# Products with v: two pairs of heads in every second unit, and the PSUM banks shared out again

## The chip, the core and the metric

One core of a Trainium2 chip runs one program. The metric is the device time of one execution in microseconds (us). Engines are named as in the profile: PE is TensorE's matmul, PEld its weight load, DVE is VectorE, ACT is ScalarE, POOL is GpSimd, SP is SyncE, which here only issues DMAs. PSUM, in which PE's results land, has eight banks; each holds 512 float32 in every partition.

## The reference

Attention with mixing of heads before and after the softmax (4 batches, 12 heads, 448 positions, head size 64), followed by a bilinear feed-forward layer:

```python
scores = scale * np.matmul(q, k.transpose(0, 1, 3, 2))
scores = np.einsum('bhij,hg->bgij', scores, w_pre)
scores = scores - np.max(scores, axis=-1, keepdims=True)
attn = np.exp(scores)
attn = attn / (np.sum(attn, axis=-1, keepdims=True) + 1e-09)
attn = np.einsum('bhij,hg->bgij', attn, w_post)
...
x = attn_out.transpose(0, 2, 1, 3).reshape(B * S, H * D)
...
a = x @ w_a
b = x @ w_b
return (a * b @ w_out).astype(np.float32)
```

## The kernel before

The first part of the kernel, up to about 360 us, is the attention. The queries of a batch are cut into chunks of 120, 120, 120 and 88, and a chunk into **units** of 20 queries (the last unit of a batch has 8). That makes 23 units a batch and 92 in all. A loop over steps (L780) runs one step for each unit, and every engine works through its instructions in the order in which this loop writes them. Step s writes, on PE:

1. `premix(s)` (L306): the heads of unit s are mixed; four matmuls, recorded as eight, into two PSUM tiles `mp`, each for 10 queries. The order is half tile 0, half tile 1, half tile 0, half tile 1. The tiles come from the pool's tag `m`, which has three banks and hands them out in turn.
2. one `qk` (L259): the scores of one pair of heads for a later chunk, eight recorded matmuls into the tile `pst`, which has one buffer of two banks.
3. `av` (L386): the product with v for one pair of heads p, 16 recorded matmuls, for a **group** of six units (120 queries; the last group of a batch has five units and 88 queries). Three pairs share the PSUM tile `xp`, p = 0 to 2 and p = 3 to 5; it has the tag `x`, which has one bank. After p = 2 and p = 5 DVE copies `xp` to `xs` (L407), and SP stores it.
4. `postmix(s-1)` (L353): the weights of unit s-1 are mixed after the softmax; 64 recorded matmuls into the two tiles `pp`, one bank each.

ACT and DVE serve this in the same step. ACT first runs `evac_p(s-2)` (L368), two copies that empty `pp`. Then for each of the two tiles `mp` DVE takes the row maximum `nm` (L327), and ACT takes the exponential `a` with the row sums (L330). The exponential is the last reader of `mp`, and so what frees its bank. ACT or DVE then empties `pst` (L278 on DVE; L280 on ACT for every third pair of heads). `norm(s)` on DVE makes the scaled mixing matrix `kr` that `postmix(s)` reads, one step later. POOL issues the DMAs that bring the mixed rows `sb` (L297) four units ahead.

The places of the products with v are a table: pair p of a group that begins with unit u0 and has n units stands in step u0 + n + `AV_AT[p]`, or `AV_SHORT[p]` for a group of five. With the old tables every step from 7 to 93 has one pair, but for the steps 25, 48 and 71, which have two. Over the whole attention there are 90 such pairs in this loop (15 groups of six); the last group comes after it.

The eight banks are: `pp` two, `pst` two, `x` one, `m` three. Besides `mp`, the tag `m` serves four `psq` tiles at the start (scores of the first chunks, L269), the sums of the last group (`xp` with a == NA - 1), and in the second part of the kernel `pa` (L599) and every second `po` (L636).

From 360 us on, the feed-forward layer runs: products `pa` and `pb` in turn, then `po`, three matmuls of 448 columns for each term.

Of the kernel before, what the change touches and what calls it, by code (L numbers as in the profile page):

```python
# [7 lines left out]
F32 = mybir.dt.float32  # L8
# [13 lines left out]
def talking_heads_bilinear_kernel(  # L22
# [12 lines left out]
    B, _, G, S = k.shape  # L35
# [14 lines left out]
    CW = KD * 128  # L50
    KH = KD // 2
    AH = 4
    AV_AT = (1, 2, 3, 4, 5, 6)
    AV_SHORT = (2, 2, 3, 4, 5, 6)
    WARM = 40
    WARM3 = 24
    QK_EARLY = 4
# [34 lines left out]
    NA = len(groups)  # L92
# [9 lines left out]
    ps = ctx.enter_context(tc.tile_pool(name="ps", bufs=2, space=PSUM))  # L102
# [28 lines left out]
    def later(fn, n=3):  # L131
        todo_at.setdefault(now[0] + n, []).append(fn)
# [15 lines left out]
    def warm_up(n):  # L148
        if not n:
            return  # L150
        t = ps.tile([128, 512], F32, tag="x", name="warm", bufs=1)
        for i in range(n):
            nc.tensor.matmul(t[:, :128], lhsT=ones, rhs=ones)

# [42 lines left out]
    st, sbt, mt, at, rss, krs, ptt, xps = {}, {}, {}, {}, {}, {}, {}, {}  # L197
# [27 lines left out]
    def cut(n):  # L225
        nb, rest = divmod(n, QB)
        return QH * nb + min(rest, QH)
# [19 lines left out]
    def qk_head(c, i, g, out):  # L247
        b, t0, n = chunks[c]
        rows = slice(D * g, D * g + D)
        h0 = cut(n)  # L250
        for e in range(2):
            cols = slice(0, 64) if e == 0 else slice(h0, n)
            nc.tensor.matmul(  # L253
                out[64 * e:64 * e + cols.stop - cols.start],
                lhsT=qt[c, i // QG][rows, i % QG, cols],
                rhs=kt[b, i][rows],
            )

    def qk(c, i, own=1):  # L259
        b, t0, n = chunks[c]  # L260
        m = 64 + n - cut(n)
        if c not in st:
            st[c] = (k_p if c % 3 == 2 else big).tile([128, H, S], F32, tag="s", name="s", bufs=1 if c % 3 == 2 else 2)
        if c <= 1 and i % 2 and i < QK_EARLY + 2 * (1 - c):
            for g in range(2):
                if i == 3:
                    sp = pp_t[g].rearrange("p x j t -> p (x j t)")[:, :S]
                else:
                    sp = ps.tile([128, 512], F32, tag="m", name="psq", bufs=3)[:, :S]  # L269
                qk_head(c, i, g, sp)  # L270
                nc.vector.tensor_copy(st[c][:m, g * G + i], sp[:m])
            return
        sp = ps.tile([128, 2, 512], F32, tag="t", name="pst", bufs=1)[:, :, :S]
        for g in range(2):
            qk_head(c, i, g, sp[:, g])
        to = st[c].rearrange("p (g i) s -> p i g s", g=2)[:m, i]
        if own:
            nc.vector.tensor_copy(to, sp[:m])  # L278
        else:
            nc.scalar.copy(to, sp[:m])  # L280

    def halves(n):
        return [(o, min(QH, n - o)) for o in range(0, n, QH)]
# [15 lines left out]
    def blocks_of(u):  # L299
        n = units[u][2]  # L300
        return [(u, j, min(QB, n - QB * j)) for j in range(2) if n > QB * j]
# [4 lines left out]
    def premix(u):  # L306
        n = units[u][2]
        tiles = sbt.pop(u)
        for k_ in blocks_of(u):
            mt[k_[:2]] = ps.tile([128, 512], F32, tag="m", name="mp", bufs=3)[:, :S]  # L310
        for i in (0, 2, 1, 3):
            if i >= len(halves(n)):
                continue
            m = halves(n)[i][1] * H
            r, col = 64 * (i // 2), 64 * (i % 2)
            M = 64 if n == QU or i == 0 else m
            nc.tensor.matmul(mt[u, i // 2][col:col + M], lhsT=wp[r:r + m, :M], rhs=tiles[i % 2][r:r + m])  # L317
# [68 lines left out]
    def av(a, p):  # L386
        b, u0, _ = groups[a]
        t0 = (u0 - b * NUB) * QU
        n = min(AVC, S - t0)
        g = p // 3  # L390
        if p % 3 == 0:
            xp = ps.tile([128, 512], F32, tag="m" if a == NA - 1 else "x", name="xp", bufs=3 if a == NA - 1 else 1)
            xps[g] = xp[:, :3 * AVC].rearrange("p (a t) -> p a t", a=3)
        xp = xps[g]
        for r in range(R):
            for e in range(2):
                h = 2 * p + e
                nc.tensor.matmul(  # L398
                    xp[64 * e:64 * e + 64, p % 3, :n],
                    lhsT=vt[b % 2][g][:C2, h % G, r],  # L400
                    rhs=ptt[a][:C2, r, h, :n],
                    start=(r == 0),
                    stop=(r == R - 1),
                )
        if p % 3 == 2:
            xs = x_p.tile([128, 3, AVC], F32, tag="xs", name="xs")
            nc.vector.tensor_copy(xs[:, :, :n], xp[:, :, :n])  # L407
            later(lambda: nc.sync.dma_start(out=xd[b][:, 3 * g:3 * g + 3, t0:t0 + n], in_=xs[:, :, :n]), 1)
# [5 lines left out]
    for c in range(1, NC):  # L414
        b, t0, _ = chunks[c]
        for i in range(G):
            j = (c - 1) * G + i
# [9 lines left out]
    for a in range(NA):  # L427
        b, u0, n = groups[a]
        for p in range(H // 2):
            av_at[a, p] = u0 + n + (AV_AT if n == GU else AV_SHORT)[p]  # L430
            if a < NA - 1:
# [146 lines left out]
    def product(f, b, e, o, k0, k1):  # L578
        hh, ll = wt["a"] if f == e == 0 else wt["f", f]
        x, off = xt[b], 0 if f == e == 0 else e * KD  # L580
        for k in range(k0, k1):
            first, last = k == 0, k == KD - 1
            nc.tensor.matmul(o, lhsT=hh[:, off + k], rhs=x[:, 0, k], start=first, stop=False)  # L583
            nc.tensor.matmul(o, lhsT=hh[:, off + k], rhs=x[:, 1, k], start=False, stop=False)  # L584
            nc.tensor.matmul(o, lhsT=ll[:, off + k], rhs=x[:, 0, k], start=False, stop=last)  # L585
# [10 lines left out]
        later(lambda: nc.sync.dma_start(out=hd[b][:, f], in_=hf), 1)  # L596

    def run_a(f, b):
        pa = ps.tile([128, 512], F32, tag="m", name="pa", bufs=3)[:, :S]  # L599
        product(f, b, 0, pa, 0, KD)  # L600
        take_a(f, b, pa)

# [29 lines left out]
    def run_o(j):  # L632
        b, m = divmod(j, KD)
        hh, ll = wt.pop(("o", j))
        th, tl = ht[b]
        po = ps.tile([128, 512], F32, tag="m" if j % 2 == 0 else f"p{j // 2 % 2}", name="po", bufs=3 if j % 2 == 0 else 1)[:, :S]  # L636
        mm3(po, hh, ll, th, tl, KF)
        so = sb_p.tile([128, S], F32, tag="sb1", name="so")
        n = S // QU * QU
        for e in range(2):  # L640
            nc.scalar.copy(
                so[:, :n].rearrange("p (u j e t) -> p u j e t", j=2, e=2, t=QH)[:, :, :, e],
                po[:, :n].rearrange("p (u e j t) -> p u e j t", j=2, e=2, t=QH)[:, :, e],
            )
        if n < S:
            nc.scalar.copy(so[:, n:], po[:, n:])
        nc.sync.dma_start(out=out[m * 128:(m + 1) * 128, b * S:(b + 1) * S], in_=so)
# [89 lines left out]
    with tc.manual_schedule():  # L737
# [6 lines left out]
        load_k(0, 3)  # L744
        act_table()
        warm_up(WARM)
        setup_mask()
        clear_v(0)
# [142 lines left out]
        for j in range(B * KD):  # L891
            b, m = divmod(j, KD)
# [57 lines left out]
```

## Time and profile before

| | |
|---|---|
| Time, median of 3 runs | 895.96 us (891.77 to 896.65) |
| Profiled execution: time | 885.13 us |
| Profiled execution: span from first to last instruction | 883.4 us |
| PE busy in the span | 862.3 us (98%) |
| DVE, ACT, POOL busy | 516.5, 376.8, 440.9 us |
| Attention loop with one pair of heads in a step (units 7 to 82) | 45.64 to 322.29 us |
| Attention loop without `qk` (units 83 to 91) and what is left of the products with v | 322.29 to some 366 us |
| Mean granted TensorE clock | 0.999 of full speed |

The profile is of one execution. A row of the timeline gives a start in us from the span's beginning and a duration in us, and merges neighbouring instructions of one kind (xcount). A matmul's recorded end is modelled, so distances are taken from start to start. PE is busy nearly throughout; what a step costs is therefore the distance from one `premix` to the next.

### The profile page before, as it was taken

The numbers are of one execution on the slowest core, as the hardware profiler recorded it, in microseconds if no ns is written. First come the engines' busy times: TensorE is split into PE (matmuls) and PEld (weight loads), VectorE is DVE, ScalarE is ACT, GpSimd is POOL, SyncE is SP. The second block draws the span as 40 slices with busy tenths as digits, with TensorE's granted clock in tenths as the row PEclk, the third lists the DMA queues.
The fourth block names the chain that finished last, engine by engine and source line by source line (L and its number), as shares of the span: only waits on it lengthen the run. The fifth ranks groups of instructions, "written<-read, shape, count | busy, mean of one in ns | idle before, by whom it ended". The sixth has DMA issues, their size and how long they took to land.

```text
span 883.4 us, 27343 instructions
## 1 busy us (share of the span) xinstructions
PE 862.3 (98%) x11440; PEld 697.7 (79%) x11440; DVE 516.5 (58%) x913; ACT 376.8 (43%) x849; POOL 440.9 (50%) x549
## 2 busy tenths in 40 slices
PE   8799999999999899999999999999999999999998
PEld 4466566566566566899999999999999989999997
DVE  5577677667777685677755566555753545151500
ACT  5677677767677677431111111111111435353421
POOL 3786868587677762044432243233322255555552
PEclk9999999999999999999999999999999999999999
DMA  7776787676777964744433333333431674747441
GB/s 203 191 201 166 198 197 189 166 197 182 199 175 196 218 173 98 235 173 164 166 122 128 131 133 138 121 121 121 139 121 50 245 263 139 264 147 269 143 144 53
DMA packets 83172, 147.47 MB, mean 167 GB/s; under 512 B 42694, under 2 KB 63026, under 8 KB 82026
## 3 DMA queue, kind: packets, MB, share of 16 engines
q1 hardware_dynamic: 54922, 108.05, 37.9%
q0 software_dynamic: 28128, 37.68, 17.3%
q8 instruction: 90, 1.47, 0.7%
q14 instruction: 32, 0.26, 0.1%
HBM read 80.23 MB, written 26.74 MB: 121 GB/s over the span
## 4 chain that ended last, share of the span: by engine, by line
PE 91%; DMA 2%; DVE 2%; ACT 1%; issue 1%; SPq 1%; POOL 1%; ACTq 0%; DVEq 0%; POOLq 0%
PE pp L362 10%; PE xp L398 10%; PE mp L317 8%; PE pst L253 8%; PE po L573 6%; PE po L574 6%; PE po L572 6%; PE pa L583 6%; PE pa L585 6%; PE pa L584 6%; PE pb L585 6%; PE pb L584 6%; PE pb L583 6%; DMA sb<-s 1%; DMA k<-in_k_dram 1%
## 5 line engine op out<-in xcount | busy, mean ns | idle before, releaser
L297 POOL DMA_DIRECT2D sb<-s x350 | 202.1, 596 | 46.1 <-PE mp L317 22.0
L524 POOL TENSOR_TENSOR cvm<-cvm,cvr 128x768 int32<-128x768 int32 (+1 forms) x37 | 66.7, 1802 | 205.3 <-DVE cvm L523 205.3
L562 POOL TENSOR_TENSOR wl<-v,wh 128x768 fp32r<-128x768 f32 x48 | 93.4, 1966 | 100.7 <-ACT wh L561 100.7
L327 DVE TENSOR_REDUCE nm<-mp 124x1 f32<-124x448 f32 x180 | 104.0, 618 | 62.5 <-PE mp L317 61.7
L330 ACT ACTIVATE a<-mp,nm 124x448 f32<-124x448 f32 x180 | 112.7, 631 | 55.7 <-DVE nm L327 55.6
L398 PEld LDWEIGHTS xp<-pt,v 120*64 120x64 f32 x1536 | 74.0, 136 | 62.8 <-issue 45.1
L589 ACT COPY sa<-pa 128x448 f32<-128x448 f32 x47 | 25.2, 536 | 213.5 <-PE pa L585 210.2
L362 PE MATMUL pp<-kr,a 60*56 60x60 f32 x5760 | 102.0, 216 | 6.0 <-issue 5.3
L377 ACT COPY pt<-pp 120x480 f32<-120x480 f32 x176 | 91.3, 575 | 38.2 <-PE pp L362 37.8
L362 PEld LDWEIGHTS pp<-kr,a 60*56 60x56 f32 x5760 | 88.4, 127 | 23.0 <-issue 12.0
L573 PE MATMUL po<-hl,wh 128*128 128x448 f32 x288 | 104.5, 363 | 0.7 <-DVE hl L630 0.7
L574 PE MATMUL po<-hh,wl 128*128 128x448 f32 x288 | 104.4, 362 | 0.0
L572 PE MATMUL po<-hh,wh 128*128 128x448 f32 x288 | 104.4, 362 | 0.0
L585 PE MATMUL pb<-xhl,wl 128*128 128x448 f32 x282 | 102.3, 363 | 0.2 <-POOL wl L562 0.2
L583 PE MATMUL pb<-xhl,wh 128*128 128x448 f32 x282 | 102.2, 362 | 0.0
L584 PE MATMUL pb<-xhl,wh 128*128 128x448 f32 x282 | 102.2, 362 | 0.0
L595 DVE TENSOR_TENSOR hf<-pb,sa 128x448 f32<-128x448 f32 x47 | 29.4, 625 | 124.4 <-PE pb L585 118.8
L630 DVE TENSOR_TENSOR hl<-hl,hh 128x448 fp32r<-128x448 f32 x48 | 57.4, 1250 | 75.9 <-ACT hh L629 75.9
L317 PE MATMUL mp<-sb,wp 60*64 60x448 f32 x720 | 96.3, 543 | 3.1 <-DMA sb<-s 2.5
L253 PE MATMUL pst<-k,q 64*64 64x448 f32 x728 | 93.6, 540 | 4.8 <-ACT s L280 1.4
L583 PE MATMUL pa<-xhl,wh 128*128 128x448 f32 x264 | 95.7, 362 | 0.0
L584 PE MATMUL pa<-xhl,wh 128*128 128x448 f32 x264 | 95.7, 362 | 0.0
(94 smaller groups left out, 1400.1 us busy)
## 6 DMA issues: line engine op xcount, KB each, us to landing
sb<-s POOLq DMA_DIRECT2D x346, 105.0 KB, 4.9
v<-wod SPq DMA_DIRECT2D x24, 768.0 KB
v<-in_w_ab_dram SPq DMA_DIRECT2D x22, 768.0 KB
hd<-hf SPq DMA_DIRECT2D x48, 224.0 KB
v<-in_w_out_dram SPq DMA_DIRECT2D x12, 768.0 KB
v<-in_v_dram SPq DMA_DIRECT2D x48, 112.0 KB
xhl<-xd SPq DMA_DIRECT2D x24, 224.0 KB
hl<-hd SPq DMA_DIRECT2D x4, 1344.0 KB
```

Of the source, the lines that this page charges most:

```text
L253: nc.tensor.matmul(out[64 * e:64 * e + cols.stop - cols.start], lhsT=qt[c, i // QG][rows, i % QG, cols], rhs=kt[b, i][rows],)
L297: (nc.sync if u <= AH and i % 2 else nc.gpsimd).dma_start(out=sbt[u][i % 2][r:r + m * H], in_=rows)
L317: nc.tensor.matmul(mt[u, i // 2][col:col + M], lhsT=wp[r:r + m, :M], rhs=tiles[i % 2][r:r + m])
L330: nc.scalar.activation(a[:m], mp[:m], ACTF.Exp, bias=nm[:m], scale=1.0, accum_out=rss[u][:m, j:j + 1])
L362: nc.tensor.matmul(pp_t[i][64 * e:64 * e + C, H * r:H * r + H, j, :m], lhsT=a[rows, keys:keys + C], rhs=kr[rows, j, :, :m],)
L398: nc.tensor.matmul(xp[64 * e:64 * e + 64, p % 3, :n], lhsT=vt[b % 2][g][:C2, h % G, r], rhs=ptt[a][:C2, r, h, :n], start=(r == 0), stop=(r ...
L572: nc.tensor.matmul(o, lhsT=hh[:, k0 + kk], rhs=mh[:, kk], start=(kk == 0), stop=False)
L573: nc.tensor.matmul(o, lhsT=hh[:, k0 + kk], rhs=ml[:, kk], start=False, stop=False)
L574: nc.tensor.matmul(o, lhsT=ll[:, k0 + kk], rhs=mh[:, kk], start=False, stop=(kk == n - 1))
L583: nc.tensor.matmul(o, lhsT=hh[:, off + k], rhs=x[:, 0, k], start=first, stop=False)
L584: nc.tensor.matmul(o, lhsT=hh[:, off + k], rhs=x[:, 1, k], start=False, stop=False)
L585: nc.tensor.matmul(o, lhsT=ll[:, off + k], rhs=x[:, 0, k], start=False, stop=last)
```

## The change

The tables become `AV_AT = (1, 1, 3, 3, 5, 5)` and `AV_SHORT = (2, 2, 4, 4, 6, 6)`: two pairs stand in every second step, and none in the steps between. The tag `x` gets two banks, so that the sums of p = 2 and p = 3, which now stand in one step, lie in different banks. The tag `m` gives up one and has two. The last group's sums move to `x`, and two of the `psq` calls at the start as well.

```diff
-    AV_AT = (1, 2, 3, 4, 5, 6)
-    AV_SHORT = (2, 2, 3, 4, 5, 6)
+    AV_AT = (1, 1, 3, 3, 5, 5)
+    AV_SHORT = (2, 2, 4, 4, 6, 6)
...
-        t = ps.tile([128, 512], F32, tag="x", name="warm", bufs=1)
+        t = ps.tile([128, 512], F32, tag="x", name="warm", bufs=2)
...
-                    sp = ps.tile([128, 512], F32, tag="m", name="psq", bufs=3)[:, :S]
+                    sp = ps.tile([128, 512], F32, tag="x" if i + c in (2, 5) else "m", name="psq", bufs=2)[:, :S]
...
-            mt[k_[:2]] = ps.tile([128, 512], F32, tag="m", name="mp", bufs=3)[:, :S]
+            mt[k_[:2]] = ps.tile([128, 512], F32, tag="m", name="mp", bufs=2)[:, :S]
...
-            xp = ps.tile([128, 512], F32, tag="m" if a == NA - 1 else "x", name="xp", bufs=3 if a == NA - 1 else 1)
+            xp = ps.tile([128, 512], F32, tag="x", name="xp", bufs=2)
...
-        pa = ps.tile([128, 512], F32, tag="m", name="pa", bufs=3)[:, :S]
+        pa = ps.tile([128, 512], F32, tag="m", name="pa", bufs=2)[:, :S]
...
-        po = ps.tile([128, 512], F32, tag="m" if j % 2 == 0 else f"p{j // 2 % 2}", name="po", bufs=3 if j % 2 == 0 else 1)[:, :S]
+        po = ps.tile([128, 512], F32, tag="m" if j % 2 == 0 else f"p{j // 2 % 2}", name="po", bufs=2 if j % 2 == 0 else 1)[:, :S]
```

What this makes of PE's order is best seen at units 59 and 60. In these rows 64x120 and 64x448 are shapes of an output, x8 merges alike instructions, and what stands in brackets is what the instruction waits for: DMASW and DMAHW are DMAs (issued by POOL and SP), Activation is ACT, DVE is DVE. The 64x120 rows are `av`, the 56x12x5 rows `postmix`.

PE at unit 59 before:

```order
L317 MATMUL mp<-sb,wp 64x448 [waits DMASW2_49]
L317 MATMUL mp<-sb,wp 64x448 [waits DMASW4_49,Activation_49]
L317 MATMUL mp<-sb,wp 64x448 [waits DMASW3_49]
L317 MATMUL mp<-sb,wp 64x448 [waits DMASW5_49]
L253 MATMUL pst<-k,q 64x448 [waits DMAHW6_49,DVE_49,Pool_49]
...
L398 MATMUL xp<-pt,v_108 64x120 [waits DVE_49,Activation_49]
L398 MATMUL xp<-pt,v_108 64x120 x7
L362 MATMUL pp_106<-kr,a 56x12x5 [waits DVE_49]
```

PE at unit 59 after:

```order
L317 MATMUL mp<-sb,wp 64x448 [waits DMASW2_49,Activation_49]
L317 MATMUL mp<-sb,wp 64x448 [waits DMASW4_49,Activation_49]
L317 MATMUL mp<-sb,wp 64x448 [waits DMASW3_49]
L317 MATMUL mp<-sb,wp 64x448 [waits DMASW5_49]
L253 MATMUL pst<-k,q 64x448 [waits DMAHW0_49,DVE_49,Pool_49]
...
L398 MATMUL xp<-pt,v_108 64x120 [waits Activation_49]
L398 MATMUL xp<-pt,v_108 64x120 x15
L362 MATMUL pp_106<-kr,a 56x12x5 [waits DVE_49]
```

The unit has 16 matmuls of the product with v (32 recorded ones) in place of 8, they no longer wait for DVE's copy of the bank, and the first matmul of `premix` has a wait for ACT that it did not have.

PE at unit 60 and the beginning of unit 61 before:

```order
L317 MATMUL mp<-sb,wp 64x448 [waits DMASW7_49]
L317 MATMUL mp<-sb,wp 64x448 [waits DMASW1_49]
L253 MATMUL pst<-k,q 64x448 [waits DMAHW7_49,Activation_49]
...
L398 MATMUL xp<-pt,v_108 64x120 x8
L362 MATMUL pp_106<-kr,a 56x12x5 [waits DVE_49,Activation_49]
L362 MATMUL pp_107<-kr,a 56x12x5 [waits Activation_49]
...
L317 MATMUL mp<-sb,wp 64x448 [waits DMASW2_49]
L317 MATMUL mp<-sb,wp 64x448 [waits DMASW4_49,Activation_49]
```

The same place after:

```order
L317 MATMUL mp<-sb,wp 64x448 [waits DMASW7_49]
L317 MATMUL mp<-sb,wp 64x448 [waits DMASW1_49]
L253 MATMUL pst<-k,q 64x448 [waits DMAHW4_49,Activation_49]
...
L362 MATMUL pp_106<-kr,a 56x12x5 [waits DVE_49,Activation_49]
L362 MATMUL pp_107<-kr,a 56x12x5 [waits Activation_49]
...
L317 MATMUL mp<-sb,wp 64x448 [waits DMASW2_49,Activation_49]
L317 MATMUL mp<-sb,wp 64x448 [waits DMASW4_49,Activation_49]
```

The unit has no product with v any more: `postmix` follows `qk`, and then comes the next `premix`, whose first matmul waits for the exponential of tile 0 of the unit just before, and whose second for that of tile 1. Before, the first bank was that of tile 1 of the unit two steps back, and the second that of tile 0 of the unit just before.

The instructions of ACT and POOL stand in the same order as before. On DVE the copies `xs` stand in other steps, and on SP some loads of k, q and v stand a step or a few earlier or later, since the planner of the loads (`plan_loads`, L434) reads the tables.

## Rows read from the trace of the kernel before

**Rows 1.** Page, part 1: busy us, share of span, instructions, by engine

```profile
PE 862.3 (98%) x11440; PEld 697.7 (79%) x11440; DVE 516.5 (58%) x913; ACT 376.8 (43%) x849; POOL 440.9 (50%) x549
```

**Rows 2.** Table by stage: stretch, length, busy of each engine, clock, DMA share, GB/s

```profile
45.64:322.29 276.65, 270.36 (x7255) 167.23 (x7250) 202.81 (x473) 197.00 (x480) 200.22 (x369) 1.00 0.76 191
322.29:360.00 37.71, 36.05 (x885) 25.00 (x875) 21.43 (x56) 24.72 (x63) 13.87 (x20) 1.00 0.56 136
```

**Rows 3.** Timeline of PE and PEld, unit 59, next premix: start, duration, instruction

```profile
233.80 0.21 PEld L317 LDWEIGHTS mp<-sb,wp 60*64 60x64 f32 x8
233.85 0.94 PE L317 MATMUL mp<-sb,wp 60*64 60x448 f32 x8
...
234.61 0.93 PE L253 MATMUL pst<-k,q 64*64 64x448 f32 x8
...
235.47 1.04 PE L398 MATMUL xp<-pt,v 120*64 120x120 f32 x16
...
236.44 1.06 PE L362 MATMUL pp<-kr,a 60*56 60x60 f32 x64
...
237.33 0.56 PE L317 MATMUL mp<-sb,wp 60*64 60x448 f32 x4
```

**Rows 4.** Timeline of PE, unit 71 (two pairs, 88 queries) and 72 (one)

```profile
276.35 0.94 PE L317 MATMUL mp<-sb,wp 60*64 60x448 f32 x8
...
277.97 1.43 PE L398 MATMUL xp<-pt,v 120*64 120x88 f32 x32
...
280.22 0.94 PE L317 MATMUL mp<-sb,wp 60*64 60x448 f32 x8
...
281.84 0.83 PE L398 MATMUL xp<-pt,v 120*64 120x88 f32 x16
...
283.48 0.56 PE L317 MATMUL mp<-sb,wp 60*64 60x448 f32 x4
```

**Rows 5.** Timeline of PE, unit 6, which has no product with v

```profile
43.91 0.98 PE L253 MATMUL pst<-k,q 64*64 64x448 f32 x8 [0.26 <-ACT s L280]
44.71 1.14 PE L362 MATMUL pp<-kr,a 60*56 60x60 f32 x61
45.64 0.54 PE L317 MATMUL mp<-sb,wp 60*64 60x448 f32 x1
```

**Rows 6.** Timeline of ACT and DVE in unit 59

```profile
234.08 1.03 ACT L377 COPY pt<-pp 120x480 f32<-120x480 f32 x2 [0.68 <-PE pp L362]
...
234.89 1.16 DVE L327 TENSOR_REDUCE nm<-mp 124x1 f32<-124x448 f32 x2
...
235.61 0.63 ACT L330 ACTIVATE a<-mp,nm 124x448 f32<-124x448 f32 x1 [0.50 <-DVE nm L327]
...
236.24 0.62 ACT L330 ACTIVATE a<-mp,nm 124x448 f32<-124x448 f32 x1
...
236.85 0.90 ACT L280 COPY s<-pst 124x896 f32<-124x896 f32 x1
```

**Rows 7.** Timeline, unit 84: a premix that waits for an exponential

```profile
324.90 0.64 ACT L330 ACTIVATE a<-mp,nm 124x448 f32<-124x448 f32 x1 [1.34 <-DVE nm L327]
...
325.68 0.20 PEld L317 LDWEIGHTS mp<-sb,wp 60*64 60x64 f32 x6 [0.52 <-ACT a L330]
...
326.58 0.20 PEld L398 LDWEIGHTS xp<-pt,v 120*64 120x64 f32 x4 [0.70 <-issue]
```

**Rows 8.** Waits of PEld, units 7 to 82: total us, times, longest

```profile
PEld xp L398 <- issue: 40.2, 58, 0.7
...
PEld pp L362 <- issue: 9.2, 28, 1.8
```

**Rows 9.** Waits in the whole span: total us, times, longest

```profile
ACT sa L589 <- PE pa L585: 210.2, 46, 6.7
...
PEld mp L317 <- ACT a L330: 2.2, 5, 0.7
...
PEld psq L253 <- DVE s L271: 0.2, 1, 0.2
```

## The prediction

> **What bounds the kernel now.** I read the page's busy times first: PE is busy 98% of the span [rows 1], so time is won or lost only on PE. The table by stage then says where the change acts. Units 7 to 82 take 276.65 us at full clock (1.00), with PE busy for 270.36; the second part of the kernel, from 360 us, has no product with v in its loop [rows 2]. A busy PE is not a PE at its peak, so I read the timeline of PE from start to start. In unit 59 the premix begins at 233.85, the scores at 234.61, the product with v at 235.47, the post-mix at 236.44 and the next premix at 237.33 [rows 3]. That is 0.76 + 0.86 + 0.97 + 0.89 = 3.48 us with no wait in it, and most units with one pair of heads and 120 queries take just that; with 88 queries a unit takes 283.48 - 280.22 = 3.26 [rows 4].
>
> Adding such undisturbed units up (58 of 3.48, 12 of 3.26, three with two pairs at 3.87 [rows 4], and three of 3.03, where the post-mix is that of a unit of 8 queries and lasts half as long) gives 261.6 us. The other 276.65 - 261.6 = 15 us are stalls that strike here and there; much of them is time in which PE's weight loads for the post-mix wait for nothing that the profile shows, 9.2 us in 28 places, up to 1.8 us [rows 8].
>
> **What the change saves on PE.** A switch to the product with v is not free. PEld stands still before it, 40.2 us in 58 places [rows 8], since its weights are loaded only when the scores are nearly through. The price of a visit comes from units that differ in nothing else. Two pairs of 88 queries take 3.87 us a unit (280.22 - 276.35) and one pair 3.26 [rows 4], so the second pair costs 0.61. A unit without the product goes from the scores to the post-mix in 44.71 - 43.91 = 0.80 [rows 5], and so would take 0.76 + 0.80 + 0.89 = 2.45 us of PE's time. Then a visit costs 3.26 - 2.45 - 0.61 = 0.20 us beside the pair itself. With 120 queries a pair is 3.48 - 2.45 - 0.20 = 0.83, and a double unit takes 3.48 + 0.83 = 4.31. There were 87 visits (90 pairs, three of them second ones) and there will be 45. Of the 42 that go, 36 lie in units 7 to 82: at 0.21 us (2 x 3.48 - 4.31 - 2.45) that is 7.6 us. I count nothing for the other six, in the stretch after 322.29, where PE waits for others anyway.
>
> **What the change adds.** The premix has two banks in place of three, and a unit needs two. So it now waits for both exponentials of the unit just before, where before its two tiles waited for an exponential two steps back and for the first of the unit before. Rows 6 give the chain. The premix of unit 59 starts at 233.85; DVE begins the two maxima at 234.89; ACT begins the first exponential at 235.61 and the second at 236.24, which ends at 236.86. That is 3.01 us after the premix began, and nothing in it depends on the product with v: DVE and ACT follow the premix, not the end of the unit. A double unit of 4.31 us hides it. An empty unit of 2.45 us does not. What such a wait costs is seen once before: in unit 84 an exponential ended at 325.54 and PEld went on at 325.68, 0.14 later; then it took 0.90 us to the next kind of work, so the premix is paid in full behind the wait [rows 7]. The weight load normally leads the premix by 0.05 [rows 3]. So an empty unit lasts 3.01 + 0.14 + 0.05 = 3.20 us, 0.75 more than PE needs. Queued behind the waiting premix are the whole next unit's scores, products and post-mix, and DVE's maxima wait for it.
>
> Units 7 to 82 get 36 empty units. Three of these are units of 8 queries with one tile, whose exponential ends some 0.6 us earlier; I take 0.1 us each. The other 33 give 33 x 0.75 = 24.8 us.
>
> [...]
>
> **What of that is hidden.** A stall of PE inside an empty unit runs beside the exponentials and is not paid twice. From the distances of the premix starts, first and last 45.64 and 322.29 [rows 2], 6.9 of the 15 us of stalls lie in units that become empty, and 5.8 of them fit under 0.75 us each. If the stalls come elsewhere this time, it is between nothing and all 15; I take 5.8, what the trace has.
>
> **Smaller terms.** In a third of the 33 empty units ACT also empties the scores (0.90 us, ending at 237.75, or 3.90 after the premix [rows 6]). The next scores would start 3.20 + 0.76 = 3.96 after it, and with the 0.14 of rows 7 they come some 0.1 us late: 11 x 0.1 = 1.1 us, between 0 and 2.5 (if the copy begins only when the row sums have been read). ACT's two copies out of `pp` then run behind this, until 1.6 us into the double unit, where the post-mix starts at 3.4: hidden. In the stretch from 322.29 to 360 [rows 2] there are no scores to cover anything, and the premix already waited for ACT five times [rows 9]; waiting for the second exponential in place of the first costs 0.62 [rows 6] at each, so 0 to 3.1 us, and I take 2. `pa` and `po` lose nothing with two banks: ACT waits for the sums (210.2 us for `pa` [rows 9]), not PE for the bank. The `psq` tiles at the start had 0.2 us of waits to lose [rows 9], and the shifted loads of k, q and v are still some units ahead of their use; both at nothing, and within 1 us either way. The DVE copies `xs` wait in the double unit for later products, but the maxima of the next unit come over 1 us after them.
>
> **Sum.** -7.6 + 24.8 + 0.3 - 5.8 + 1.1 + 2 = +14.8 us. Against the profiled execution's own 885.13 us (span 883.4, 1.7 around it) that is 899.9. The three runs have a median 10.8 us above that execution; I put the difference on the median: 895.96 + 14.8 = **911**. Bounds of this case: all 15 us of stalls absorbed and the small terms at nothing gives +2.5, none absorbed and the small terms full gives 24.8 + 0.3 - 7.6 + 2.5 + 3.1 = +23, so 899 to 919.
>
> **Rivals.** *Only the saving stays.* If the exponentials were through when the next premix comes, 42 visits x 0.21 = 8.8 us would be won: 887. It decides at 2.45 us from premix to the end of the second exponential; for it speaks that PE is all that counts, against it that the rows show 3.01 in unit 59 and that the chain has no slack in it to lose, since the 0.5 us before each exponential is its wait for DVE. [...] Chance 0.07.
>
> *The stalls make room.* PE's stalls come from deliveries that have their own pace (DMA share 0.76 in this stage [rows 2]); a stage that runs slower may lose nearly all 15 us of them, and then the waits only take their place: -7.6 + 25.1 - 15 = +2.5, or 898.5. Against it: more than half of the stalls strike units that become double, where nothing waits. Chance 0.12.
>
> *Double units wait too.* If ACT, pushed back by the empty unit, is late in every double unit, for the scores' tile or for `pp`, each pair of units costs another 0.2 us, and no stall is absorbed: 25.1 - 7.6 + 36 x 0.2 + 2.5 + 3.1 = +30, or 926. For it speaks that ACT's work is 3.4 us in the units where it empties the scores; against, that over two units it has 7.5 us for some 6. Chance 0.12.
>
> That the change doesn't do what it says I rule out: the order shows the pairs moved and the waits added.
>
> **How the numbers follow.** The forecast, 911, has 0.69. A measurement of this kernel tells about 0.5%, 4.5 us, from no change. Faster by more than that is the first rival alone, 0.07. Within it, below 900.4, are most of the second rival and the lowest edge of the forecast: 0.11. Slower: 0.82. The range for 8 in 10 is 900 to 922: it leaves out the first rival, part of the second and most of the third.
>
> **What would show it.** In the trace after, premix starts should alternate: some 3.2 us for an empty unit, 4.3 for a double one, 7.5 a pair against 6.96; PEld should wait for the exponential (`mp` for ACT `a`) some 30 to 38 times for about 0.7 us, 25 us in all, where it had 2.2. The product with v should go from 16 to 32 in a row with 1.8 us to the post-mix. From the end of the attention on, all distances should be as before. If empty units take 2.5 us, the wait that I rest on is not there; if double units take over 4.5, ACT is the bound.

## The result, and the profile after

| | before | after |
|---|---|---|
| Median, us | 894.39 (20 runs, 887.77 to 906.81) | 900.12 (20 runs, 894.31 to 906.87) |
| Profiled execution: time, span | 885.13, 883.4 | 900.64, 898.9 |

The ratio is 1.0074, 95% interval 1.005 to 1.0099: the changed kernel is slower by 6.6 us (4.5 to 8.9). Sign and reason were forecast; the size was not: +14.8 us were predicted. The forecast had been 911, with 900 to 922 for 8 in 10; the 900.12 lie on the lowest edge of that range. The changed kernel does not lie 15.5 us behind, as the two profiled executions do: that profile of before is 9 us below the median of its kernel. Ratios, here and below, compare the fast executions of both kernels taken side by side, as some executions of any kernel here take 1 or 2% longer, so a ratio need not be the quotient of two medians.

PE is still busy 98% of the span. Part 1 of the page after (busy us, share, instructions; [rows 1] before):

```profile
PE 878.4 (98%) x11440; PEld 722.0 (80%) x11440; DVE 516.1 (57%) x913; ACT 375.6 (42%) x849; POOL 441.0 (49%) x549
```

The table by stage after answers to [rows 2] (length, then the busy time of PE, PEld, DVE, ACT and POOL, clock, DMA share, GB/s). Units 7 to 82, the rest of the attention, the products `pa` and `pb`, and the products `po`:

```profile
45.57:332.09 286.52, 280.74 (x7271) 192.09 (x7264) 201.86 (x475) 195.59 (x480) 201.41 (x370) 0.99 0.75 184
332.09:376.46 44.37, 42.36 (x985) 30.66 (x973) 25.15 (x63) 29.99 (x74) 13.12 (x19) 1.00 0.59 149
376.46:715.48 339.02, 338.78 (x1694) 317.59 (x1693) 208.54 (x271) 54.57 (x91) 110.51 (x58) 1.00 0.40 141
715.48:898.90 183.42, 178.79 (x865) 161.31 (x863) 53.74 (x43) 66.86 (x154) 88.98 (x46) 1.00 0.48 171
```

Units 7 to 82 take 286.52 us in place of 276.65, with PE's busy time 10 us longer. The last stage is 5.6 us longer too, but that is not the change (see the last section).

PE's timeline from unit 58 to the premix of unit 62 (start, duration, instruction) answers to [rows 3]:

```profile
239.82 0.55 PE L317 MATMUL mp<-sb,wp 60*64 60x448 f32 x1
...
240.59 1.08 PE L253 MATMUL pst<-k,q 64*64 64x448 f32 x8
241.35 1.17 PE L362 MATMUL pp<-kr,a 60*56 60x60 f32 x64
242.46 1.59 PE L317 MATMUL mp<-sb,wp 60*64 60x448 f32 x8
243.55 1.25 PE L253 MATMUL pst<-k,q 64*64 64x448 f32 x8
244.73 1.86 PE L398 MATMUL xp<-pt,v 120*64 120x120 f32 x32
246.52 1.06 PE L362 MATMUL pp<-kr,a 60*56 60x60 f32 x64
247.41 1.04 PE L317 MATMUL mp<-sb,wp 60*64 60x448 f32 x8
...
249.99 1.22 PE L317 MATMUL mp<-sb,wp 60*64 60x448 f32 x5
...
254.94 1.00 PE L317 MATMUL mp<-sb,wp 60*64 60x448 f32 x8
```

Units now alternate: unit 60, without a product, lasts 249.99 - 247.41 = 2.58 us, units 59 and 61, with two pairs, 4.95 each, so a pair of units takes 7.5. The product is 32 rows long and 1.79 us stand between it and the post-mix. ACT over the same place shows who holds the premix back:

```profile
241.68 0.64 ACT L330 ACTIVATE a<-mp,nm 124x448 f32<-124x448 f32 x1 [0.52 <-DVE nm L327]
...
242.30 0.62 ACT L330 ACTIVATE a<-mp,nm 124x448 f32<-124x448 f32 x1
...
249.21 0.64 ACT L330 ACTIVATE a<-mp,nm 124x448 f32<-124x448 f32 x1 [0.54 <-DVE nm L327]
```

The first exponential of unit 58 ends at 242.32, and 0.14 later, at 242.46, the first matmul of the next premix starts; the first exponential of unit 60 ends at 249.85, and again 0.14 later, at 249.99, comes the next one. The second tile waits for the second exponential (242.92), and the scores come at 243.55, 0.63 after it. So the wait has two parts: a little at the end of the empty unit, the larger part inside the premix at the head of the double unit. PEld's waits in units 7 to 82 (total us, times, longest) show the same; [rows 8] before:

```profile
PEld xp L398 <- issue: 24.0, 33, 1.4
...
PEld pp L362 <- issue: 14.5, 60, 2.1
PEld mp L317 <- ACT a L330: 12.2, 29, 0.5
PEld pst L253 <- ACT s L280: 6.5, 11, 0.6
```

The wait of the scores for ACT's copy out of `pst` had been, in the kernel before:

```profile
PEld pst L253 <- ACT s L280: 5.9, 18, 0.7
```

The wait in front of the product with v has fallen from 40.2 us in 58 places to 24.0 in 33. New are the 12.2 us for the exponential. The scores' wait for ACT's copy is not new in its sum: 5.9 us in 18 places have become 6.5 in 11, 0.6 each, all in double units. It costs little beside the other wait, as these units last 5.00 in place of 4.95 us, or 4.57 in place of 4.52.

**How many stalls are left.** The prediction's step, adding up units as long as they are where nothing odd happens, was repeated. Before they give 261.7 us. After, a double unit takes 4.95 behind an empty one with 120 queries, 4.52 with 88, 4.03 behind a short unit and 4.36 behind another double one; an empty unit takes 2.54, a short one 2.35. With 24 x 4.95 + 9 x 4.52 + 3 x 4.03 + 4 x 4.36 + 33 x 2.54 + 3 x 2.35 that is 279.9 us, or +18.2. What a profile has beyond it is counted as stalls. Two more profiles of each kernel were taken. The stage in the second and third profile, first of the kernel before, then of the changed one:

```profile
47.04:329.81 282.77, 270.55 (x7256) 167.83 (x7250) 203.20 (x473) 196.96 (x480) 198.03 (x365) 1.00 0.76 186
47.44:328.21 280.77, 271.32 (x7254) 167.41 (x7249) 202.33 (x473) 197.44 (x480) 199.32 (x365) 0.99 0.76 187
```

```profile
45.77:331.83 286.06, 279.36 (x7272) 192.33 (x7264) 201.68 (x475) 195.53 (x480) 200.47 (x370) 1.00 0.75 185
46.50:334.80 288.30, 281.41 (x7271) 194.53 (x7264) 201.83 (x475) 195.42 (x480) 199.72 (x369) 1.00 0.73 183
```


| units 7 to 82, us | length | undisturbed | stalls |
|---|---|---|---|
| before, as shown ahead | 276.6 | 261.7 | 15.0 |
| before, second | 282.8 | 261.7 | 21.1 |
| before, third | 280.8 | 261.7 | 19.1 |
| after, as shown here | 286.5 | 279.9 | 6.6 |
| after, second | 286.1 | 279.9 | 6.2 |
| after, third | 288.3 | 279.9 | 8.4 |

The stage is longer by 287.0 - 280.1 = 6.9 us in the mean, close to the 6.6 us of the timed runs. Undisturbed, it is 18.2 us longer, and the stalls give 11.3 of that back.

**What the stalls are.** The timeline of PE and PEld, in the kernel before, in unit 76 (297 us):

```profile
296.97 0.51 PEld L362 LDWEIGHTS pp<-kr,a 60*56 60x56 f32 x32 [0.16 <-issue]
296.98 0.64 PE L362 MATMUL pp<-kr,a 60*56 60x60 f32 x31
299.23 0.65 PE L362 MATMUL pp<-kr,a 60*56 60x60 f32 x33 [1.62 <-issue]
299.23 0.51 PEld L362 LDWEIGHTS pp<-kr,a 60*56 60x56 f32 x32 [1.75 <-issue]
```

In the middle of a post-mix, which is one run of alike instructions, PE stands still for 1.62 us, and the profile names nothing that it waited for (`issue`). The DMA view of the kernel before has a queue of instruction transfers (packets, MB, share of the DMA engines), here over the whole span:

```profile
q8 instruction: 90, 1.47, 0.7%
```

That is 16.4 KB a packet. PE and PEld have 22,880 instructions together, and with the waits that are recorded for PEld 23,155 records, 90.4 times 256. Counting all these records from the first, every gap of over 0.3 us inside a post-mix of the attention from 45 to 330 us lies at number 193 or 194 modulo 256 (all 10 in the profile of before, all 6 in that of after), and ends 1.3 to 2.0 us after a packet of this queue has landed. I take these stalls for PE's next 256 instructions coming late. That one packet brings them is my reading of the counts, 90 packets for 90.4 blocks; what fills the time from its landing to the end of the gap is not shown, and in two of these four rows the packet had landed before the gap began:

```text
before: gap from   to       us     number  modulo 256   packet starts, lands
            95.21   96.42   1.22    4033      193          93.40    94.80
           206.44  207.29   0.85    9922      194         204.94   205.89
           297.40  299.23   1.83   14785      193         296.57   297.92
after:     176.03  178.24   2.21    8130      194         175.92   176.90
```

The other boundaries bear this out. In units 7 to 82 each boundary has one packet of its own, in all six profiles. Blocks that were late begin 1.5 us after their packet landed in the mean; those that were not, 2.1 us after it in the kernel before and 2.6 us in the changed one.

### The profile page after: what moved, and what is told of

The parts are those of the page before. It is cut to its first block, busy times and chain, and to the rows that moved or that the text cites. A ratio compares the mean times of both kernels' runs of the same rounds, so it can differ in the third digit from the quotient of the medians.

```text
span 898.9 us, 27427 instructions
## 1 busy us (share of the span) xinstructions
PE 878.4 (98%) x11440; PEld 722.0 (80%) x11440; DVE 516.1 (57%) x913; ACT 375.6 (42%) x849; POOL 441.0 (49%) x549
## 3 DMA queue, kind: packets, MB, share of 16 engines
q8 instruction: 90, 1.47, 0.7%
## 4 chain that ended last, share of the span: by engine, by line
PE 91%; DVE 3%; ACT 2%; DMA 2%; issue 1%; POOL 1%; SPq 0%; ACTq 0%; DVEq 0%
PE mp L317 10%; PE xp L398 9%; PE pp L362 9%; PE pst L253 8%; PE po L573 6%; PE po L572 6%; PE po L574 6%; PE pa L583 6%; PE pa L584 6%; PE pa L585 6%; PE pb L585 6%; PE pb L584 6%; PE pb L583 6%; DMA sb<-s 1%; ACT s L280 1%
## 5 line engine op out<-in xcount | busy, mean ns | idle before, releaser
L362 PEld LDWEIGHTS pp<-kr,a 60*56 60x56 f32 (+1 forms) x5760 | 97.3, 127 | 30.1 <-issue 17.1
L317 PE MATMUL mp<-sb,wp 60*64 60x448 f32 x720 | 115.6, 558 | 4.3 <-DMA sb<-s 2.4
L253 PE MATMUL pst<-k,q 64*64 64x448 f32 (+2 forms) x728 | 106.2, 547 | 4.0 <-ACT s L280 1.5
L377 ACT COPY pt<-pp 120x480 f32<-120x480 f32 x176 | 91.0, 575 | 44.6 <-PE pp L362 44.2
L362 PE MATMUL pp<-kr,a 60*56 60x60 f32 (+1 forms) x5760 | 102.0, 215 | 5.5 <-issue 4.3
```

What stands on the lines that cost most here:

```text
L253: nc.tensor.matmul(out[64 * e:64 * e + cols.stop - cols.start], lhsT=qt[c, i // QG][rows, i % QG, cols], rhs=kt[b, i][rows],)
L362: nc.tensor.matmul(pp_t[i][64 * e:64 * e + C, H * r:H * r + H, j, :m], lhsT=a[rows, keys:keys + C], rhs=kr[rows, j, :, :m],)
```

## Experiments

**The kernel before and the changed kernel, unchanged, for a second profile.**

> The kernel before once more, unchanged, for a second profile. Two things are open in the difference of the first two profiles (+15.5 us): 9.8 us lie in units 7 to 82 (276.65 against 286.5 us), 5.6 us in the products po, whose matmuls came every 200 ns before and every 206.7 ns after. Theory A (an execution of the kernel before usually has more stalls in units 7 to 82 than the 15 us of the first profile, and the change hides them): units 7 to 82 take 279 to 281 us. Theory B (the stage is always some 277 us, and the difference to the timed runs lies elsewhere): 276 to 277.5 us. On po: if the slower pace belongs to the change, 200 ns here; if it belongs to an execution, either.

> The changed kernel once more, unchanged. Theory A and theory B: units 7 to 82 take 285 to 288 us, pairs of units 7.5 us. On po: if the slower pace belongs to the change, 206.7 ns again; if it belongs to an execution, it may be 200 ns, and the time then is about 5.6 us shorter.

One execution each, 892.75 and 894.70 us. The stage took 282.8 and 286.1 us, the first above the 279 to 281 of theory A and far from theory B, the second as expected. So the 9.9 us between the first two profiles were 3.3 this time, and the reason stands in the table above: the stalls of before had been 15.0 and were 21.1, those of after 6.6 and 6.2. The product `po` took 177.9 us in both.

**A third profile of each.**

> The kernel before unchanged, a third profile: units 7 to 82 take 279 to 286 us, of which 18 to 24 us are stalls. If the 15 us of the profile that the prediction read were the usual amount, 275 to 278.

> The changed kernel unchanged, one more profile: units 7 to 82 take 285 to 289 us, of which 6 to 9 us are stalls. If the first two profiles were lucky, 290 or more.

280.8 and 288.3 us: stalls of 19.1 and 8.4, both within what was expected. The profile that the prediction had read was the one with the fewest stalls.

**The banks alone.** The old tables, with the new banks (the edit is against the changed kernel).

```diff
-    AV_AT = (1, 1, 3, 3, 5, 5)
-    AV_SHORT = (2, 2, 4, 4, 6, 6)
+    AV_AT = (1, 2, 3, 4, 5, 6)
+    AV_SHORT = (2, 2, 3, 4, 5, 6)
```

> The banks as after (x two, m two), the products with v in their old places, one pair in each unit. My theory (the wait for both exponentials costs only where a unit is shorter than 3.2 us): units of 3.48 and 3.26 us hide it, only the three units of 3.03 us lose 0.2 us each, so the time is that of before within 2 us, and units 7 to 82 take some 277 us. Rival (three banks are needed for any unit, since the premix then has no slack for late exponentials): 5 to 10 us slower.

899.25 us, ratio 1.0011 (0.9972 to 1.0049). Two banks for the premix cost nothing that the timed runs can tell where every unit has a product with v: in [rows 6] the second exponential ended 3.01 us after the premix began, and a unit here takes 3.54 us. The wait of the premix for ACT was 0.3 us in units 7 to 82. The stage itself was not the 277 us that I expected:

```profile
45.62:335.44 289.82, 277.33 (x7255) 182.19 (x7246) 202.89 (x474) 197.40 (x480) 200.19 (x369) 0.99 0.74 183
```

A unit took 3.54 us in place of 3.48, the difference lying between scores and product (0.93 for 0.86); why is open. So the undisturbed units add up to 266.3 us in place of 261.7, and the other 23.5 us are stalls.

**The tables alone, with three banks for the premix.** The sums of two pairs share a tile, so that one bank serves them; with it, DVE's copies to `xs` and their stores become three smaller ones a group in place of two. The main lines of the edit, against the changed kernel:

```diff
+        g, d = p // 3, p // 2
+        if p % 2 == 0:
+            xp = ps.tile([128, 512], F32, tag="m" if a == NA - 1 else "x", name="xp", bufs=3 if a == NA - 1 else 1)
...
-            mt[k_[:2]] = ps.tile([128, 512], F32, tag="m", name="mp", bufs=2)[:, :S]
+            mt[k_[:2]] = ps.tile([128, 512], F32, tag="m", name="mp", bufs=3)[:, :S]
```

> The places as after (two pairs in every second unit), but the banks as before (x one, m three): each double unit has a sum of its own for its two pairs, emptied by DVE at its end, so that one bank does for x. My theory: the premix after an empty unit waits only for the first exponential (2.40 + 0.14 after the premix), so an empty unit takes 2.45 to 2.6 us in place of 3.2. Then the scores' tile is next: where ACT empties it in an empty unit (one in three) the double unit takes some 5.1 us, else 4.5; a pair takes 7.0 to 7.6, 7.2 in the mean, against 7.5 after and 6.96 before. Time: before + 0 to 5 us. Rival (the banks don't matter; two pairs in a row are what costs): as after, + 6 to 7 us, with pairs of 7.5 us.

891.39 us, ratio 0.9956 (0.992 to 0.9991): now it is faster, where I expected 0 to 5 us more than before. Where the gain lies is not shown: in its profile units 7 to 82 took 279.6 us, as the 280.1 of before. PE's timeline (start, duration, instruction):

```profile
232.15 0.96 PE L317 MATMUL mp<-sb,wp 60*64 60x448 f32 x8
...
234.50 1.16 PE L317 MATMUL mp<-sb,wp 60*64 60x448 f32 x8
235.44 0.98 PE L253 MATMUL pst<-k,q 64*64 64x448 f32 x8
...
239.02 0.94 PE L317 MATMUL mp<-sb,wp 60*64 60x448 f32 x8
```

An empty unit takes 2.35 us and a double one 4.52, together 6.87, where two units of before took 6.96. With `banks_only` this shows that neither edit by itself costs anything that the timed runs can tell, and that the loss of the change is the wait that they make together. Of the 0.21 us of saving per visit only 0.09 are left here, since the double unit's premix still takes 0.94 us to the scores (234.50 to 235.44) in place of 0.76. By the order of the banks its second tile has the one that the first exponential of the unit before reads; that this is the cause is my reading, as the list of waits has the premix wait for ACT's exponential only twice up to 330 us (1.4 us). Where ACT copies `pst` in the empty unit, the double unit takes 5.18.

**That copy moved to the double units**, beside the edit above, by ACT emptying `pst` in these alone (`doubles` holds the first step of each two pairs):

```diff
-                    it += (it[2] % OWN if s not in late else 1,)
+                    it += (0 if s in doubles else 1,)
```

> As three_banks, and ACT empties the scores in the double units, DVE in all others (before: ACT for every third pair of heads). In three_banks the double units after an empty one took 5.18 us where ACT had emptied the scores in the empty one, and 4.53 to 4.57 else. My theory (the wait that is left after the banks are back is that for the scores' tile): no double unit of 5.18 any more, a pair takes 2.35 + 4.53 = 6.88 us against 6.96 before, and three_banks loses 0.2 us a pair or 7 to 8 us, of which stalls give back up to half: 0.3 to 0.8% faster than three_banks. Rival (ACT in the double units delays the exponentials there, or the copies out of pp): pairs stay at 7.1 us and the time at that of three_banks.

892.69 us, ratio 0.9972 (0.9942 to 1.0003). The units of 5.18 us are gone, and units 7 to 82 took 277.0 us in the profile, 259.2 of them undisturbed; but against the kernel with three banks alone the 0.3 to 0.8% that I expected can't be told in the timed runs.

**The product with v ahead of the scores in a double unit**, beside both edits above.

```diff
-            for it in items.get(s, ()):
+            first = s in doubles and all(it[0] is not av or it[2] for it in items[s])
+            for it in sorted(items.get(s, ()), key=lambda it: it[0] is qk) if first else items.get(s, ()):
```

> As act_in_doubles, and in the double units that don't need the newest copies of pp (the second and third of a group) the two products with v stand ahead of the scores, so that the scores' tile has 1.8 us more to be emptied. My theory: these double units take 4.3 us in place of 4.53, 24 x 0.2 = 5 us less without stalls, so 2 to 5 us faster than act_in_doubles. Rival (the products wait where the scores did, for ACT's copies or for the switch of tiles): no gain, double units of 4.5 us.

892.28 us, ratio 0.9925 (0.9889 to 0.9961). The double unit still took 4.53 us and not the expected 4.3, so the order was not what it waits for. A second series was run, since the gain was greater than the units explain:

> products_first unchanged, for a second series. If the gain is the kernel's, the ratio to before is again 0.989 to 0.996 and units 7 to 82 take 275 to 280 us; if it was that series, it is within 0.3% of 1.

890.42 us, ratio 0.9971 (0.9943 to 1.0). So this kernel, too, came out a few tenths of a per cent faster than before, the second time with an interval that reaches 1, and which of the three is best was not settled. The last stage alone differs by 5.5 us between executions of one kernel (last section), as much as these gains.

**The exponentials freed from the maximum.** On both kernels the exponential takes a bias of zero; the maximum is still computed, but no longer subtracted.

```diff
-        nc.scalar.activation(a[:m], mp[:m], ACTF.Exp, bias=nm[:m], scale=1.0, accum_out=rss[u][:m, j:j + 1])
+        nc.scalar.activation(a[:m], mp[:m], ACTF.Exp, bias=zero[:m], scale=1.0, accum_out=rss[u][:m, j:j + 1])
```

> The changed kernel, but the exponentials take a constant zero in place of the row maximum as bias, so that they needn't wait for DVE (the maximum is still taken, and the softmax is the same in exact arithmetic, since its sums divide the factor out). The second exponential then ends some 2.55 us after the premix (ACT's copies out of pp end at 1.3, then two of 0.63) in place of 3.01, so a pair of units without stalls takes some 7.05 us in place of 7.5, 15 us less over 33 pairs. Theory A (waits and stalls hide each other: with less waiting, more stalls show): of these 15 us only 4 to 9 are won, that is 891 to 896 us where after has 900, units 7 to 82 some 278 to 282 us, with 10 to 17 us of stalls in place of 6.5. Theory C (the stalls of the changed kernel are few because its order is kind to them, whatever waits there are): all 15 us won, 885 us, units 7 to 82 some 271 us, with 6.5 us of stalls.

> The kernel before with the same edit, as the control: its premix waits for no exponential, so the edit frees nothing: the time of before within 2 us, units of 3.48 us as they were, under theory A and under theory C. If it is faster by more than 3 us, the edit itself brings something that has nothing to do with the premix's wait.

Ratios 1.005 (1.0015 to 1.0084) and 1.0012 (0.9971 to 1.0054), 899.37 and 898.96 us: as without the edit. It missed its aim. DVE and ACT in the changed kernel with the edit:

```profile
242.85 1.16 DVE L327 TENSOR_REDUCE nm<-mp 124x1 f32<-124x448 f32 x2 [1.24 <-PE mp L317]
...
243.57 0.64 ACT L330 ACTIVATE a<-mp,zero 124x448 f32<-124x448 f32 x1 [0.50 <-DVE nm L327]
```

The exponential reads nothing of `nm` any more and still waits 0.50 us for DVE's maximum: it waits on a semaphore that DVE raises. Both read the same PSUM tile, so the program probably keeps the two in order for that; this was not tested. So whether a shorter chain would give the wait back was not tested. As a fourth pair of profiles the two give 285.5 us for units 7 to 82 before, more than in any of the three, and 288.2 after: again more stalls before (23.9 us) than after (8.3).

**The wait without the double units.** `banks_only`, with two more ACT copies between the exponentials of 33 units, about every second one; `held(u)`, left out here, picks them. This is the run that tells two explanations of the missing stalls apart: they fell because the product's order changed, or because a wait and a late instruction block hide each other.

```diff
+        if j == 1 and held(u):
+            for _ in range(2):
+                nc.scalar.copy(a[:m, :350], zero[:m].to_broadcast([m, 350]))
         nc.scalar.activation(a[:m], mp[:m], ACTF.Exp, bias=nm[:m], scale=1.0, accum_out=rss[u][:m, j:j + 1])
```

> banks_only once more (old tables, one pair in each unit, two banks for the premix), with two extra ACT copies of 350 columns between the two exponentials of 33 units of units 8 to 82, about every second one. Their result is overwritten by the second exponential, so nothing of the output changes. At some 0.56 us each (0.62 for an exponential of 448 columns, 0.90 for a copy of 896, about 0.0006 us a column) the second exponential should end about 4.1 us after the premix began, and the next premix come at about 4.3 in place of 3.54: a wait of some 0.75 us in 33 units, 25 us, placed much as the change places it, but with no double unit and with PE's instructions as in banks_only. The theory that such waits and PE's late instructions hide each other: stalls at instruction blocks fall from banks_only's 23 us to some 8 to 12, and the kernel is 10 to 16 us slower than banks_only, a ratio to before of 1.012 to 1.019. Rival, the stalls fell with the changed kernel because two pairs stand together (other instructions at other places), and a wait hides none of them: the full 22 to 27 us, a ratio of 1.026 to 1.031.

903.55 us, ratio 1.0121 (1.0063 to 1.0179). ACT and PE (start, duration, instruction) in a held unit and the next:

```profile
234.48 0.99 ACT L338 COPY a<-zero 124x350 f32<-124x350 f32 x2
...
235.50 0.63 ACT L339 ACTIVATE a<-mp,nm 124x448 f32<-124x448 f32 x1
...
236.19 0.54 PE L317 MATMUL mp<-sb,wp 60*64 60x448 f32 x1
...
237.07 0.98 PE L253 MATMUL pst<-k,q 64*64 64x448 f32 x8
```

PEld's waits of units 7 to 82 (total us, times, longest), and the table by stage:

```profile
PEld mp L317 <- ACT a L339: 14.4, 30, 0.7
```

```profile
45.63:338.98 293.35, 288.14 (x7256) 178.15 (x7247) 202.72 (x474) 225.75 (x546) 198.97 (x368) 1.00 0.71 180
```

The two copies took 0.99 us and not 1.1, and the wait came out smaller than I had put it: an undisturbed held unit and its successor take 3.54 + 4.09 in place of 2 x 3.54, so 0.55 us, and 0.77 with 88 queries (4.10 for 3.33). With 24 units of the first kind and 9 of the second that is 20 us over the undisturbed 266.3 of `banks_only`. If the stalls had stayed, the ratio would be 1.0011 + 20/895 = 1.023, above the interval. Measured are 1.0121 - 1.0011 = 0.011, or about 10 us (4 to 16, from the two intervals), the low end of the 10 to 16 that I expected. In the two profiles the stage is 293.35 against 289.8, so stalls of 7 us against 23.5. No product was moved here: the waits alone did it.

Counted apart, this is the time that PE lost at the boundaries of its blocks of 256 instructions in units 7 to 82 (excess over the usual distance of the same two instructions; of some 58 boundaries a profile, those that were late by over 0.15 us):

| mean of a profile | late | us |
|---|---|---|
| no wait, one pair a unit: before (three profiles) and `banks_only` | 22 | 16.5 |
| no wait, two pairs: `three_banks`, `act_in_doubles`, `products_first` (two) | 22 | 19.1 |
| wait, two pairs: after (three) and `no_max_after` | 14 | 9.7 |
| wait, one pair: `wait_added` | 13 | 9.7 |

(`no_max_before` isn't in the first row. Other ways of taking the usual distance move the totals by about 2 us, and leave the contrast.) At places 64 or 128 records away from the boundaries the same count gives 0 to 2 us in each of the kernels. The wait makes the difference, not the places of the products.

## Why the prediction was wrong in size

- **The saving.** Two units of 3.48 were to become 4.31 + 2.45 us of PE's time. Where nothing waits, it is 2.35 + 4.52 (`three_banks`), 0.09 saved a pair of units and not 0.21: the premix takes 0.2 us longer even with three banks (0.94 us to the scores for 0.76). In the changed kernel itself this is inside the next point.
- **The wait.** Predicted 7.51 us a pair of units; measured 2.54 + 4.95 = 7.49. The chain of [rows 6] and the 0.14 us of [rows 7] held to a few hundredths. That the wait would stand as one piece in the empty unit was wrong: the first tile's bank comes free 0.6 us before the second's, so the first matmuls start at 2.54 and the rest of the wait stands in the next unit. The list of waits names only 12.2 us of it, and not 25, since half appears as a longer way from premix to scores (1.09 us, 242.46 to 243.55, for 0.76) and to the product (1.18 for 0.86); only the distance from premix to premix has all of it.
- **The saving, the wait and the scores' tile together.** Predicted -7.6 + 24.8 + 0.3 + 1.1 = +18.6 us for undisturbed units; measured 279.9 - 261.7 = +18.2.
- **What of that is hidden** is the step that failed. I took 5.8 us, from the places that the stalls had in one profile. In the mean of three profiles each the stalls fell from 18.4 to 7.1 us, so the change got 11.3 back. By the table above 6.8 of these (16.5 - 9.7) are blocks that come late less often (14 in place of 22), for which the prediction had no term; the other 4.5, by subtraction and so only to about 2 us, ran beside a wait, which is what the 5.8 stood for. Two errors are in it. The profile had 15.0 us, the fewest of three, and I added the difference to a median whose executions had more. And I held the number and the places of the stalls for given: more than half of them, I wrote, strike units that become double, where nothing waits. But the double unit has the longer part of the wait at its head, and late blocks are rare behind it: over the four profiles with the wait, 79 block boundaries fell into the post-mix of a double unit and 6 were late, 1.1 us a profile. In the post-mix of the empty units 22 of 68 were late, 5.0 us a profile, and such a stall runs beside the exponentials.
- **Smaller terms.** For the stretch behind unit 82 I took 2 us; from unit 83 to the first `pa` it was 44.1, 44.2 and 44.4 us before, 44.4, 44.0 and 44.9 after: 0.2. `pa` and `pb` took 339.0 us in all six: nothing, as said.
- **Sum.** +18.2 - 11.3 + 0.2 = +7.1 us, against the measured 6.6 (4.5 to 8.9). That is closer than three profiles a kernel can promise, with 276.6 to 282.8 us for the same stage before.
- **The rivals.** *The stalls make room* (898.5) had nearly the right outcome, with 11.3 us of stalls gone where it had all 15, and in outline the right mechanism, as `wait_added` shows that waits take the stalls' place; I had set it at 0.12 because the stalls' places spoke against it. *Only the saving stays* fell with the exponentials of 242.92 and the premix behind them. *Double units wait too* is there for the scores' tile, 0.6 us in each of 11 places, but nearly all of it falls together with the other wait: these units are 0.05 us longer, some 0.5 us in all (counted above among the stalls), so my 1.1 us was rather too high.

That blocks come late less often where PE has other waits (13 a profile in place of 22) is shown by `wait_added`, with the products in their old places. Of how that comes about the traces show a part. Counted from the first record of a block, the next block's packet starts after 1.87 us in the mean of the three profiles before and after 1.43 in the changed kernel, 2.02 in `banks_only` and 1.51 in `wait_added`. The blocks themselves last only 0.1 us longer (4.88 and 4.97; 5.02 and 5.08), and from start to landing the packet takes 1.2 us in all of them. So the packet starts earlier relative to PE's work, rather than PE reaching the boundary later; what makes it start earlier is open.

## What to carry to other kernels

Before charging a new wait in full, look at what the stalls of the waiting engine are: here those at the boundaries of PE's instruction blocks became fewer where PE had other waits (22 late blocks a profile, then 13 or 14), and a wait of 18 us cost 7. A bank count is to be read against the length of the unit that has to cover it: two banks cost nothing that the timed runs could tell (ratio 1.0011) under a unit of 3.5 us, and made PE wait at every second unit when one of 2.45 was made. Take the baseline of a sum from two or three profiles: this kernel's own executions (887.77 to 906.81 us) differ by more than the whole effect.

## What the runs showed of the hardware

- **Late instruction blocks.** With one pair in each unit PE lost 16.5 us a profile (first row of the table above) at the boundaries of its blocks of 256 instructions, up to 2.5 us at a time (unit 58 in the third profile of the kernel before), with 1.47 MB in 90 packets on that queue. About 22 of some 58 boundaries were late, and late blocks began 1.5 us after their packet had landed in the mean.
- **Two paces of the last stage.** The products `po` of 448 columns had a mean of 362 ns in most profiles and of 367 ns in others, and from start to start 200.0 and 206.5 ns, at a granted clock of 1.00 in both. Grouped by shape, 715 us to 800 us, in the second profile of the changed kernel and in the first (count, busy us, mean ns):

```profile
L572 PE MATMUL po<-hh,wh 128*128 128x448 f32 x141 | 51.1, 362 | 0.0
```

```profile
L572 PE MATMUL po<-hh,wh 128*128 128x448 f32 x136 | 49.9, 367 | 0.0
```

  The stage takes 177.9 or 183.4 us by that. It is of the execution and not of the kernel: the slower pace was also in a profile of `no_max_before`, whose `po` code is that of before, and the faster one in two of the three profiles of the changed kernel. What sets it is open.
